# An adaptive-norm block on one core: block transposition over two banks, normalisation on VectorE alone, modulation on VectorE and ScalarE, and another order of the work

## Chip, core and metric

The kernel runs on one core of a Trainium2 chip. The metric is the device time of one execution in microseconds (us). Before the change, five runs took 339.01, 339.18, 339.24, 340.96 and 343.09 us; the median is 339.24.

## What is computed

One row of S = 2048 tokens with D = 640 goes through a transformer block whose scales, shifts and gates come from a condition vector c:

```python
mod = (_silu(c) @ w_mod).reshape(c.shape[0], 6, 1, -1)
sa, ca, ga, sb, cb, gb = (mod[:, 0].copy(), mod[:, 1].copy(), mod[:, 2].copy(), mod[:, 3].copy(), mod[:, 4].copy(), mod[:, 5].copy())
h = _layernorm(x, axis=-1) * (1 + ca) + sa
x = x + ga * _A_ref(h, A_wqkv, A_wo)
h = _layernorm(x, axis=-1) * (1 + cb) + sb
x = x + gb * _B_ref(h, B_w_gate, B_w_up, B_w_down)
```

`_A_ref` is causal attention with 32 heads of 20 and a window of 256 keys. `_B_ref` is a gated layer of width 1536: `sigmoid(h @ w_gate) * (h @ w_up) @ w_down`. Inputs and output are bf16.

## The kernel before

The tokens are cut into 8 chunks of 256, each of two blocks of 128. For a chunk a the work is:

- `ln1` loads the two blocks of x (`load_x`), takes mean and variance (`ln_stats`: bn_stats and bn_aggr on VectorE, L741 and L743), the power -1/2 on GpSimd (POOL, L746 and L748), and normalises in place, (x - mean) * r, at L751. For chunks 0 and 1 the normalised blocks are transposed on TensorE and modulated while they leave PSUM (L786, L787). For chunks 2 to 7 they are transposed by a DMA (L757) into hT, and then modulated there, five instructions a chunk, 256 columns each (`modulate`, L765 on ScalarE, L766 on VectorE or POOL). hT has two buffers.
- `qkv` multiplies hT by the weights of Q, K and V, in groups of five matmuls of 320 columns (`pe_chain`, L658). ScalarE or VectorE copies each group out of PSUM (`evac`, L812 and L813). Q and K are transposed, on TensorE in chunks 0 and 1 (tags qtr, then the copies evqt), by DMA after that.
- `attention` goes through the chunk in two halves of the heads. A half has six sets (three in chunk 0). A set is 8 or 16 score matmuls into the one PSUM tile S (L659), one exponential of 128 x 2048 on ScalarE (L924), and masks on POOL (L932, L934). When all sets of a half are there, a burst of 64 matmuls (32 in chunk 0; "PV") multiplies them by V into two neighbouring PSUM banks X (`burst`).
- `norm` divides the half by its sum: X is transposed in blocks of 32 x 32 into T1 (L975, one instruction for each bank), reciprocal (L980), product (L982), and a transposition back, into On (L984). Four DMAs store it and one loads it again as oT.
- `outproj` multiplies oT by wo and adds x (L1038), then a second norm with the same `ln_stats`, a DMA transposition into h2T and `modulate`. `mlp` runs gate and up matmuls of 256 columns, tanh on ScalarE (L1078), the gated product on VectorE (L1080), the down matmuls, and the addition of x (L1099). Then the block is stored.

PSUM holds S (four banks) and four banks M, which all other groups share, X among them. The gates are multiplied into wo (L1123) and wd (L1064) on VectorE. The three parts of w_mod are loaded into the buffers of wd, wu and hh and multiplied by silu(c) (tags modA, modb, modc).

The order is made when the kernel is built. `Prog.op` records each operation with the engines that may do it, a duration for each, what it reads and writes, and a priority; `Prog.schedule` then places them one after another. It takes, for each engine, the operations that could start within a small margin of the earliest (`PE_EPS` for TensorE, 0.04 for the others), picks of them the one with the lowest priority number, and puts it on the engine where it can start first. A priority is the number written at the call plus the entry of its tag in the table `PRI`:

```python
o.prio = prio + PRI.get(tag, 0.0)
```

Each engine then runs its list strictly in that order, with semaphores between engines. Nearly all DMAs are issued from SP's queue, in such an order too; the bulk loads of weights are chained, so that each waits for the third before it. `port=True` marks operations of VectorE that the placing keeps apart from POOL's. `PACE0` and `PACE` give an earliest time to score sets. The constants that the change touches stand at L399 to L461: `TR1` (used in `norm`, L974 and L977), `XHE` (engines for L751) and `MOE` (engines for `modulate`).

Of the kernel before, what the change touches and what calls it, by code (L numbers as in the profile page):

```python
# [80 lines left out]
class Prog:  # L81
# [67 lines left out]
    def schedule(self):  # L149
# [70 lines left out]
        while placed < n:  # L220
            best = None
            for e in ENGS:
# [21 lines left out]
                if not lst:  # L244
                    continue
                eps = PE_EPS if e == "pe" else 0.04
                pick = min((x for x in lst if x[0] <= tmin + eps), key=lambda x: (x[1].prio, x[1].seq))
# [147 lines left out]
def c_pe(n):  # L395
    return max(n, 64) / 2400.0 + 0.0027


PE_EPS = 0.117  # L399
PRI = {  # L400
    "amodu2": 349.1, "amodu3": 69.8, "amodu4": -2, "amodu5": 20.4, "amodu6": 21.9, "amodu7": 33.4, "apow0": -17.1,
    "apow1": -0.2, "apow2": -233.1, "apow3": -9.4, "apow4": -4.7, "apow5": -39.6, "apow6": -201.2, "apow7": 26.9,
    "astats1": 2, "astats2": -137.3, "astats3": 147.7, "astats4": 52, "astats5": 202.7, "astats6": 112.2,
    "astats7": -8.8, "atr3": -6.2, "atr4": -3.2, "atr5": -194.6, "atr6": 10.3, "atr7": -24.5, "axh0": -203,
    "axh2": -66.7, "axh3": 71.6, "axh4": -24.4, "axh5": 33.9, "axh6": -20.5, "axh7": 9.8, "bmodu0": -166.8,
    "bmodu1": 13.9, "bmodu2": 1.5, "bmodu3": 15.4, "bmodu4": -1.8, "bmodu5": 93.1, "bmodu6": 3.4, "bmodu7": -1.2,
    "bpow0": 4.3, "bpow1": 150.8, "bpow2": -11.8, "bpow3": -188.6, "bpow4": -35, "bpow5": 41.6, "bpow6": -22.5,
    "bpow7": -15.1, "bstats0": 20.1, "bstats1": 21.9, "bstats2": 16.8, "bstats3": 14.9, "bstats4": 25.8,
    "bstats5": -84.4, "bstats6": 22.4, "bstats7": -22.6, "btr0": -39.2, "btr1": -39.3, "btr2": -8.5, "btr3": 35,
    "btr5": -82, "btr6": 4.1, "btr7": -2.4, "bxh0": 24.8, "bxh1": -260.1, "bxh2": -55.1, "bxh3": 34, "bxh4": 72.4,  # L410
    "bxh5": 103.8, "bxh6": 81, "bxh7": 17.1, "divide_0": -16.1, "divide_1": 34.3, "divide_2": -154.9,
    "divide_3": 6.6, "divide_4": 14.8, "divide_5": -19.9, "divide_6": -11.9, "divide_7": 6.6, "down0": -15.1,
    "down1": -21.3, "down2": -20, "down4": 0.4, "down5": 1.9, "down7": 60.2, "evqk0": 16.1, "evqk1": 334.5,
    "evqk2": 27.2, "evqk3": 339.9, "evqk4": -0.3, "evqk5": 4.1, "evqk6": -33, "evqk7": -0.3, "evqt0": -11.6,
    "evqt1": -8.4, "evv0": 41.8, "evv1": 235.3, "evv2": 2.5, "evv3": -5.5, "evv4": -16.9, "evv5": -108.2,
    "evv6": -60.1, "evv7": -59.5, "exp0": -116.1, "exp1": -16.2, "exp2": -46.3, "exp3": 5.9, "exp4": -147.4,
    "exp5": -3.4, "exp6": 1.1, "exp7": -126.7, "glu_0": -1.3, "glu_1": 0.5, "glu_2": 26.7, "glu_3": -19.5,
    "glu_4": -37, "glu_5": -3.6, "glu_6": 8.5, "glu_7": 4.2, "hTe0": -31.6, "hTe1": 34.3, "mask0": 136.2,
    "mask2": -61.4, "mask3": 78.7, "mask4": -36.4, "mask5": -30.5, "mask6": 3.2, "mask7": 94.8, "mlpg0": -25,
    "mlpg1": -24.5, "mlpg2": -24, "mlpu0": -25, "mlpu1": -24.5, "mlpu2": -24, "modb": -25.7, "modc": -22.2,  # L420
    "n_ow_0": -20.3, "n_ow_1": -41.5, "n_ow_2": 44.8, "n_ow_3": 103.9, "n_ow_4": -5.8, "n_ow_5": -19.8,
    "n_ow_6": -1.4, "n_ow_7": 33.8, "oT_0": 17.5, "oT_1": 32.5, "oT_2": 12.6, "oT_3": 76.6, "oT_4": -64.2,
    "oT_5": 13.2, "oT_6": 2.6, "oT_7": 49.3, "out": 7.2, "projk0": -33.4, "projk2": 26.4, "projk3": -3.9,
    "projk4": 15.6, "projk5": 1.5, "projk6": 7.4, "projk7": 4, "projq0": -114.6, "projq2": 45.3, "projq3": -8.2,
    "projq4": 6.1, "projq5": -4, "projq6": 8.5, "projq7": -7.9, "projv0": -43.1, "projv1": 8.7, "projv2": 224.6,
    "projv4": -6, "projv5": 2.7, "projv6": 16.2, "projv7": 10.7, "ptr0": -337.9, "ptr1": -256.9, "pv0": -37.3,
    "pv1": -290.4, "pv2": -37.9, "pv3": -37.1, "pv4": -28.1, "pv5": -70.8, "pv6": -10.1, "pv7": -9.1, "qkt2": 7.9,
    "qkt3": 6.7, "qkt4": 64.8, "qkt5": -12.3, "qkt6": -3.6, "qkt7": -4.9, "qtr0": -154.4, "qtr1": -20.9,
    "recip_1": -1.9, "recip_2": 23.6, "recip_3": -2.4, "recip_4": 28.1, "recip_5": -22.7, "recip_6": 2.1,
    "recip_7": -9.2, "res1_0": -0.2, "res1_1": 5, "res1_2": 55.2, "res1_3": 7.6, "res1_4": 13.1, "res1_5": -5.3,  # L430
    "res1_6": -6.4, "res1_7": 11.2, "res2_0": 6.2, "res2_1": -29.9, "res2_2": -5.9, "res2_3": 1.7, "res2_4": -3.1,
    "res2_5": 40.9, "res2_6": -17.8, "res2_7": 2.6, "score0": -287.1, "score1": -347.7, "score2": -20.2,
    "score3": 1.8, "score4": -13.1, "score5": -50.5, "score6": -2.7, "score7": 11.5, "tanh_0": 29, "tanh_1": 20.7,
    "tanh_2": 23.5, "tanh_3": 22.7, "tanh_4": 26.2, "tanh_6": -2.3, "tanh_7": -20.3, "tr1_0": 19.8, "tr1_1": 6.2,
    "tr1_2": -28.1, "tr1_3": 15.6, "tr1_4": 45.4, "tr1_5": -90.8, "tr1_6": -19.7, "tr1_7": 5.2, "tr2_0": 204.6,
    "tr2_1": 224.6, "tr2_2": -128.4, "tr2_3": 42, "tr2_4": 64.5, "tr2_5": 40.4, "tr2_6": 0.1, "tr2_7": 27.5,
    "wd": -19.6, "wds": -7.7, "wg": 2.8, "wm2": -13.2, "wo": -20, "wo0": -2.2, "wo1": -12.2, "wo2": 9.1, "wo4": 10.8,
    "wo5": 28.7, "wo6": 6.6, "wo7": 30, "wos": -29.2, "x10": 529.8, "x11": 584.9, "x12": 476, "x13": 633,
    "x14": 745.4, "x15": 731.1, "x4": 394.6, "x5": 337, "x6": 375.5, "x7": 0.5, "x8": 473.6, "x9": 471.4, "y0": 10.9,
    "y1": 23.7, "y10": 8.6, "y11": 0.3, "y12": 0.2, "y13": 31.2, "y14": 1, "y15": 2.7, "y2": -0.2, "y3": 0.4,  # L440
    "y4": 24.5, "y5": 24.4, "y6": 15.9, "y7": -3, "y8": 23.9, "y9": 2,
}
TR1 = 2
NPH = 2
NPQ = 2
DEEP = 3
MW = 64
PACE0 = -95.83
PACE = 0.103
AFTER = 0  # L450
LEAD = 2
FILL = 1
# [4 lines left out]
QMAX = 4.5  # L457
PAIR = 0
PAIRO = 0
XHE = ('dve', 'pool')  # L460
MOE = ('dve', 'act', 'pool')  # L461


def build(nc, A_x, A_wqkv, A_wo, B_x, B_w_gate, B_w_up, B_w_down, c, w_mod, out, S=2048):
# [268 lines left out]
    def ln_stats(src, dst, prio, ln, a):  # L733
# [3 lines left out]
        def v(lo, w):  # L737
            return st.ap[:, lo:lo + w]
# [11 lines left out]
        for bi in range(n):  # L750
            A(XHE, lambda e, g, bi=bi: e.tensor_scalar(dst[bi].ap[:], src[bi].ap[:], v(24 + 2 * bi, 1), v(30 + bi, 1),  # L751
                                                       op0=ALU.subtract, op1=ALU.mult), {"dve": 0.44, "pool": 0.95}, port=True,
# [7 lines left out]
    def modulate(dst, sc, sh, Rmod, prio, ln, a):  # L760
        for dt in range(NDT):
            def mo(e, g, dt=dt):
# [3 lines left out]
                return e.tensor_scalar(ap, ap, sc[:, dt:dt + 1], sh[:, dt:dt + 1], op0=ALU.mult, op1=ALU.add)  # L766
            A(MOE, mo, {"dve": 0.34, "act": 0.59, "pool": 0.55}, port=True, reads=[dst.r(("t", bi)) for bi in range(2)] + Rmod, writes=[dst.r(dt)],prio=prio, tag=f"{ln}modu{a}")

# [202 lines left out]
    def norm(X, On, a):  # L971
        T1, Tn, Dr = Tile(p_T1, "T1"), Tile(p_Tn, "Tn"), Tile(p_Dr, "Dr")
        blk = lambda t: t.ap[:].rearrange("p (b r) -> p b r", r=32)[:, :, 0:DH]
        for h in range(2) if TR1 == 2 else ():  # L974
            A("dve", lambda e, g, h=h: e.transpose(T1.ap[:, 512 * h:512 * h + 512], X[h].ap), 0.694, reads=[X[h].r()],  # L975
              writes=[T1.r(h)], prio=3.5, tag=f"tr1_{a}")
        if TR1 == 1:  # L977
            A("dve", lambda e, g: e.transpose(T1.ap[:], Mall[:, X[0].slot:X[0].slot + 2, :].rearrange("p a c -> p (a c)")), 1.23,
# [9 lines left out]
    def attention(a):  # L988
# [20 lines left out]
        for q in range(2):  # L1009
            sets = plan(a)  # L1010
            Es = []
            for si, (ps, md, mf) in enumerate(sets):
                Es.append(score_set(a, q, si, ps, md, mf, PACE0 + PACE * nset[0] if a else 0.0))
                nset[0] += 1
# [167 lines left out]
```

The softmax here doesn't subtract the row's maximum and nothing guards it: scores larger than these inputs give would overflow.

## Time and profile before

The profiled execution took 339.54 us. Its span, from the first to the last instruction of the program, is 337.6 us.

| | busy us | share of the span | instructions |
|---|---|---|---|
| TensorE, matmul (PE) | 327.7 | 97% | 4146 |
| TensorE, weight load (PEld) | 233.1 | 69% | 4146 |
| VectorE (DVE) | 222.2 | 66% | 441 |
| ScalarE (ACT) | 230.0 | 68% | 220 |
| GpSimd (POOL) | 184.1 | 55% | 255 |

| group | count | mean ns |
|---|---|---|
| exponential, ACT, L924 | 90 | 1877 |
| normalisation on DVE, L751 | 26 | 633 |
| normalisation on POOL, L751 | 6 | 2525 |
| modulation of hT on DVE, ACT, POOL | 11, 10, 9 | 611, 591, 576 |
| modulation of h2T on DVE, ACT, POOL | 18, 14, 8 | 429, 590, 564 |
| transposition of one bank, DVE, L975 | 32 | 694 |
| transposition back, DVE, L984 | 16 | 1233 |

How to read it: times are in us unless marked ns. A line such as L751 is a line of the kernel; PE, PEld, DVE, ACT and POOL are the engines, SPq is the queue of DMAs. `x2` counts instructions. In a timeline a row has start, duration, engine, line, operation, what it writes and reads, and in brackets how long the engine stood before it and for whom. A group's "idle before" is the time in which its engine stood just ahead of it. Matmuls are pipelined and their ends are modelled, so a TensorE that is marked busy can still be slower than it could be. The granted clock is the share of TensorE's full clock.

### The profile page before, as it was taken

To read this page: it belongs to the slowest core of one execution; us is meant where nothing else is said; L and a number is where in the kernel's file an instruction comes from. 1 tells how busy PE (TensorE), PEld (TensorE's weight loads), DVE (VectorE), ACT (ScalarE), POOL (GpSimd) and SP (SyncE) were. 2 spreads that over 40 slices of the span, in tenths; PEclk is the share of its full clock that TensorE was granted. 3 is DMA by queue.
4 is the path that set the end of the run, shared out by engine and by line. 5 is a ranking of instruction groups with operands and counts; after the bars stand their busy time and mean duration, and the time that the engine had idled before them with its cause. 6 is when DMAs were issued, how large, how long until landed. Compare 5 with 4: busy or idle time off the path is not lost.

```text
span 337.6 us, 10119 instructions
## 1 busy us (share of the span) xinstructions
PE 327.7 (97%) x4146; PEld 233.1 (69%) x4146; DVE 222.2 (66%) x441; ACT 230.0 (68%) x220; POOL 184.1 (55%) x255
## 2 busy tenths in 40 slices
PE   8998979999999999999999999999999999999996
PEld 3665646666776667766677666776677788887885
DVE  4597768889799767366897376844667662733332
ACT  1597769888998498968799779998699532230120
POOL 4138899775869686656686556665576610100000
PEclk9999979999999999999999999999999999999999
DMA  7988999787980287116871426100140231101101
GB/s 263 375 271 286 249 310 166 139 186 96 231 240 10 67 141 123 46 56 132 119 122 41 91 73 136 39 17 21 60 95 25 60 91 48 21 19 41 41 0 39
DMA packets 71686, 38.72 MB, mean 115 GB/s; under 512 B 46682, under 2 KB 68442, under 8 KB 71642
## 3 DMA queue, kind: packets, MB, share of 16 engines
q1 hardware_dynamic: 71344, 37.76, 46.6%
q8 instruction: 32, 0.52, 0.7%
q10 hardware_dynamic: 298, 0.33, 0.3%
q14 instruction: 12, 0.10, 0.1%
HBM read 21.96 MB, written 5.24 MB: 81 GB/s over the span
## 4 chain that ended last, share of the span: by engine, by line
PE 78%; POOL 9%; DMA 7%; DVE 3%; issue 2%; ACT 1%; ACTq 0%; SPq 0%; POOLq 0%
PE M L658 65%; PE S L659 7%; PE M L659 6%; POOL x L751 3%; DMA x<-in_A_x_dram 3%; POOL E L934 3%; POOL E L932 2%; DMA wo<-in_A_wo_dram 2%; DMA hT<-x 1%; DMA hh<-in_w_mod_dram 1%; ACT E L924 1%; DVE st L741 1%; POOL st L748 1%; DVE x L751 1%; DVE x L1099 0%
## 5 line engine op out<-in xcount | busy, mean ns | idle before, releaser
L924 ACT ACTIVATE E<-S 128x2048 bf16<-128x2048 f32 x90 | 168.9, 1877 | 32.3 <-PE S L659 29.0
L932 POOL TENSOR_SCALAR_AFFINE_SELECT E<-E 128x512 bf16<-128x512 bf16 (+2 forms) x90 | 76.1, 846 | 71.8 <-ACT E L924 68.0
L934 POOL TENSOR_SCALAR_AFFINE_SELECT E<-E 128x512 bf16<-128x512 bf16 (+1 forms) x84 | 69.4, 826 | 0.0
L658 PE MATMUL M<-h2T,wg 128*128 128x256 bf16 x480 | 63.6, 273 | 0.1
L658 PE MATMUL M<-h2T,wu 128*128 128x256 bf16 x480 | 63.2, 273 | 0.0
L1080 DVE SCALAR_TENSOR_TENSOR hh<-sig,M 128x512 bf16<-128x512 f32 x48 | 32.5, 680 | 46.0 <-PE M L658 30.8
L1078 ACT ACTIVATE sig<-M 128x512 f32<-128x512 f32 x48 | 28.5, 594 | 43.9 <-PE M L658 43.9
L658 PE MATMUL M<-wd,hh 128*128 128x320 bf16 (+2 forms) x396 | 55.6, 295 | 0.0
L658 PEld LDWEIGHTS M<-h2T,wg 128*128 128x128 bf16 x480 | 45.0, 98 | 9.6 <-issue 3.0
L658 PEld LDWEIGHTS M<-h2T,wu 128*128 128x128 bf16 x480 | 45.9, 98 | 7.4 <-issue 1.7
L658 PEld LDWEIGHTS M<-wd,hh 128*128 128x128 bf16 x396 | 37.0, 98 | 15.4 <-issue 1.7
L659 PE MATMUL S<-QT,KT 20*128 20x256 bf16 (+1 forms) x960 | 36.1, 246 | 1.8 <-DVE KT L813 1.8
L741 DVE BATCH_NORM_STATS2 st<-x 128x6 f32<-128x320 bf16 x64 | 28.1, 477 | 3.6 <-DMA x<-in_A_x_dram 3.1
L1099 DVE TENSOR_TENSOR x<-M,x 128x320 bf16<-128x320 f32 (+2 forms) x33 | 15.5, 477 | 22.4 <-PE M L658 22.4
L659 PEld LDWEIGHTS S<-QT,KT 20*128 20x128 bf16 x960 | 14.1, 92 | 22.3 <-ACT E L924 16.3
L975 DVE STREAM_TRANSPOSE T<-M 128x512 f32<-128x512 f32 x32 | 21.2, 694 | 12.5 <-PE M L659 12.4
L658 PE MATMUL M<-wk,hT 128*128 128x320 bf16 x160 | 27.1, 309 | 0.0
L658 PE MATMUL M<-wq,hT 128*128 128x320 bf16 x160 | 25.5, 299 | 0.1
L658 PE MATMUL M<-wv,hT 128*128 128x320 bf16 x160 | 25.1, 300 | 0.0
L658 PE MATMUL M<-wo,oT 128*128 128x320 bf16 x160 | 24.7, 300 | 0.0
L659 PE MATMUL M<-E,V 128*32 128x256 bf16 (+1 forms) x960 | 22.8, 246 | 1.4 <-POOL E L934 0.7
L659 PEld LDWEIGHTS M<-E,V 128*32 128x32 bf16 x960 | 20.0, 97 | 5.7 <-issue 2.2
(76 smaller groups left out, 323.2 us busy)
## 6 DMA issues: line engine op xcount, KB each, us to landing
x<-in_A_x_dram SPq DMA_DIRECT2D x30, 160.0 KB
doc<-On SPq DMA_DIRECT2D x64, 40.0 KB
out_dram<-x SPq DMA_DIRECT2D x15, 160.0 KB
wg<-in_B_w_gate_dram SPq DMA_DIRECT2D x5, 384.0 KB
wu<-in_B_w_up_dram SPq DMA_DIRECT2D x5, 384.0 KB
wd<-in_B_w_down_dram SPq DMA_DIRECT2D x4, 480.0 KB
wd<-in_w_mod_dram SPq DMA_DIRECT2D x5, 320.0 KB
wu<-in_w_mod_dram SPq DMA_DIRECT2D x5, 320.0 KB
```

The costliest lines, as they stand in the source:

```text
L658: return e.matmul(o, l, r, start=st, stop=sp, skip_group_check=True)
L659: return e.matmul(o, l, r, start=st, stop=sp, tile_position=tp, skip_group_check=True)
L741: A("dve", lambda e, g, bi=bi, j=j: e.bn_stats(v(bi * 12 + j * 6, 6), src[bi].ap[:, j * 320:(j + 1) * 320]), 0.48, reads=[src[bi].r()], wr ...
L748: A("pool", lambda e, g: e.tensor_tensor(v(30, n), v(28, n), mhalf[:, 0:n], op=ALU.pow), 0.71, reads=[st.r("v"), R_mh], writes=[st.r("r")] ...
L751: A(XHE, lambda e, g, bi=bi: e.tensor_scalar(dst[bi].ap[:], src[bi].ap[:], v(24 + 2 * bi, 1), v(30 + bi, 1), op0=ALU.subtract, op1=ALU.mul ...
L924: A("act", lambda e, eng: e.activation(E.ap[:], Sp.ap[:], ACT.Exp, scale=SM_SCALE), 1.876, reads=[Sp.r()], writes=[E.r()], prio=3, tag=f"e ...
L932: return e.affine_select(ap, ap, pattern=[[0, ap.shape[1]], [1, 128]], compare_op=ALU.is_ge, fill=0.0, base=0, channel_multiplier=-1)
L934: return e.affine_select(ap, ap, pattern=[[0, ap.shape[1]], [-1, 128]], compare_op=ALU.is_ge, fill=0.0, base=-1, channel_multiplier=1)
L975: A("dve", lambda e, g, h=h: e.transpose(T1.ap[:, 512 * h:512 * h + 512], X[h].ap), 0.694, reads=[X[h].r()], writes=[T1.r(h)], prio=3.5, t ...
L1078: A("act", lambda e, g, pg=pg, sg=sg: e.activation(sg.ap[:], pg.ap[:], ACT.Tanh, scale=0.5), c_act(512), reads=[pg.r()], writes=[sg.r()], ...
L1080: A("dve", lambda e, g, pu=pu, sg=sg, f0=f0: e.scalar_tensor_tensor(out=hh.ap[:, f0:f0 + 2, :], in0=sg.ap[:].rearrange("p (a b) -> p a b", ...
L1099: A("dve", lambda e, g, ps=ps, bi=bi, c0=c0, n=n: e.tensor_tensor(x1[bi].ap[:, c0:c0 + n], ps.ap[:, 0:n], x1[bi].ap[:, c0:c0 + n], op=ALU. ...
```

## The change

Three options, three constants and the whole table of priorities change. `TR1 = 1` makes `norm` transpose both banks of X in one VectorE instruction of 1024 columns, in place of one of 512 for each bank. `XHE = ("dve",)` lets only VectorE normalise. `MOE = ("dve", "act")` lets only VectorE and ScalarE modulate. All other operations are the same, on the same engines to choose from; every engine's order is remade, since the table is another one.

```diff
-PE_EPS = 0.117
+PE_EPS = 0.116
...
-TR1 = 2
+TR1 = 1
 NPH = 2
 NPQ = 2
 DEEP = 3
 MW = 64
-PACE0 = -95.83
-PACE = 0.103
+PACE0 = -178.4
+PACE = -4.513
...
-XHE = ('dve', 'pool')
-MOE = ('dve', 'act', 'pool')
+XHE = ("dve",)
+MOE = ("dve", "act")
```

The table has some 200 entries. Those that the prediction speaks of, as the sum of the number at the call and the entry (lower goes first):

| operation (tag) | before | after |
|---|---|---|
| copy of transposed Q or K, chunk 1 (evqt1) | 5 - 8.4 = -3.4 | 5, no entry |
| transposition back, chunk 0 (tr2_0) | 4 + 204.6 = 208.6 | 4 + 13 = 17 |
| statistics of the first norm, chunk 4 (astats4) | 14 + 52 = 66 | 14 - 82.2 = -68.2 |
| load of x for block 6 (x6) | 0.55 + 375.5 = 376.1 | 0.55 + 1.9 = 2.5 |
| load of x for block 7 (x7) | 0.55 + 0.5 = 1.05 | 0.55 + 435.6 = 436.2 |
| load of x for block 8 (x8) | 20.4 + 473.6 = 494 | 20.4 + 850.9 = 871.3 |
| load of the second part of w_mod (wm1) | 0.4, no entry | 0.4 + 79.8 = 80.2 |
| gate and shift products (modb, first and second) | 18 - 25.7 = -7.7, 19 - 25.7 = -6.7 | 40.3, 41.3 |
| the same as columns (modc, first and second) | 18 - 22.2 = -4.2, 19 - 22.2 = -3.2 | 42.3, 43.3 |
| projection of Q, chunks 1 and 3 to 6 | 21, 14.8, 30.1, 21, 34.5 | 52.4, 72.3, 164.8, 126.8, 97.2 |
| projection of K, chunks 1 and 3 to 6 | 21, 19.1, 39.6, 26.5, 33.4 | 57, 55.1, 101.8, 15.9, 206.2 |
| gate and up matmuls, chunks 0 to 7 | 15, 16.5, 18, 43 to 47 | the same |

## Prediction

> **What bounds the kernel now.** I read the page first: busy time, then the slices.
>
> ```profile
> span 337.6 us, 10119 instructions
> ...
> PE 327.7 (97%) x4146; PEld 233.1 (69%) x4146; DVE 222.2 (66%) x441; ACT 230.0 (68%) x220; POOL 184.1 (55%) x255
> ...
> PE   8998979999999999999999999999999999999996
> ...
> PEclk9999979999999999999999999999999999999999
> ```
>
> TensorE is busy in 97% of the span, the others idle a third of it or more. But matmuls are pipelined, and a busy mark is not full speed; so I read the windows next (columns: stretch, length, then busy time and count of PE, PEld, DVE, ACT, POOL, then granted clock, DMA share, GB/s) and counted matmuls.
>
> ```profile
> 40.00:50.00 10.00, 8.20 (x77) 4.58 (x74) 6.91 (x13) 7.27 (x9) 8.30 (x14) 0.83 1.12 335
> ...
> 100.00:110.00 10.00, 10.00 (x110) 6.96 (x109) 9.93 (x22) 8.57 (x7) 10.00 (x11) 1.00 0.05 13
> ...
> 130.00:140.00 10.00, 10.00 (x126) 7.76 (x124) 4.99 (x8) 9.89 (x9) 5.95 (x8) 1.00 0.51 94
> ```
>
> ```profile
> 40.00:45.00 5.00, 3.62 (x34) 2.13 (x31) 3.98 (x6) 4.48 (x6) 3.83 (x8) 1.00 1.05 373
> 45.00:50.00 5.00, 4.58 (x43) 2.45 (x43) 2.93 (x8) 2.79 (x3) 4.47 (x7) 0.66 1.19 296
> ```
>
> Full speed comes from the tail, where TensorE does gate and up matmuls alone: in the timeline one group of 10 starts every 1.09 us (318.46, 319.55, 320.64), 0.109 us for 256 columns, 0.426 ns a column. A matmul of 320 columns is then 0.136 us, one of 128 is 0.055. A score set of 8 or 16 matmuls is a 0.33 us piece in the chain, a PV burst 1.43 to 1.50. In 130 to 140 us TensorE does 38 gate and 38 up matmuls (8.28 us) and 48 score matmuls (4.5 sets, 1.5 us): 9.8 of 10. In that steady state there is nothing to gain. In 40 to 50 us it does 35 projection matmuls (4.77), 8 transposing ones (0.44) and 3 score sets (1.0): 6.2 of 10, so 3.8 us are lost, though "busy" says 8.20. The same count for the other start slices gives 8.6, 8.4, 7.7 and 9.2 of 10 for 10 to 20, 20 to 30, 30 to 40 and 50 to 60 us: 1.4, 1.6, 2.3 and 0.8 lost. So 9.9 us can be won back before 60 us, and hardly anything behind it. A loss can be put anywhere. The timeline of the hole:
>
> ```profile
> 34.22 2.43 SPq L536 DMA_DIRECT2D wg<-in_B_w_gate_dram  x2
> ...
> 36.74 1.21 SPq L757 DMA_TRANSPOSE hT<-x  x1
> ...
> 41.62 1.10 POOL L766 TENSOR_SCALAR hT<-hT,mA 128x256 bf16<-128x256 bf16 x2 [1.17 <-issue]
> ...
> 42.76 0.89 DVE L741 BATCH_NORM_STATS2 st<-x 128x6 f32<-128x320 bf16 x2 [1.02 <-DMA x<-in_A_x_dram]
> ...
> 43.56 1.23 DVE L984 STREAM_TRANSPOSE On<-Tn 128x1024 bf16<-128x1024 bf16 x1
> ...
> 44.71 0.65 DVE L813 CAST KT<-M 128x512 bf16<-128x512 f32 x1
> ...
> 45.42 0.40 PE L659 MATMUL S<-QT,KT 20*128 20x128 bf16 x16 [1.80 <-DVE KT L813]
> ...
> 46.44 1.26 PE L658 MATMUL M<-wk,hT 128*128 128x320 bf16 x4
> ...
> 49.20 5.00 POOL L751 TENSOR_SCALAR x<-x,st 128x640 bf16<-128x640 bf16 x2
> ...
> 60.26 1.50 PE L659 MATMUL M<-E,V 128*32 128x256 bf16 x64 [0.75 <-POOL E L934]
> ```
>
> On the way in, chunk 2's two transposing transfers are issued at 32.80 (right behind its normalisation on POOL, 30.18 to 32.77) and at 36.74 (behind two weight loads on SP's queue, 34.22 to 36.65); they land at 41.5, and POOL modulates from 41.62 to 47.48, in turn with masks. In the hole itself VectorE stands in order: it waits 1.02 us for x of chunk 4 (42.76), does a transposition (1.23 us), and only then the copy of K, 44.71, that the next score set waits for (1.80 us). With projections of chunk 2 behind that set in its own order, TensorE stands, and the granted clock falls to 0.66 in 45 to 50 us. Last, two normalisations hold POOL for 5.0 us from 49.20, the masks queue behind them, and the PV burst at 60.26 waits 0.75 us for a mask. The groups (busy time, mean ns, then idle before):
>
> ```profile
> L975 DVE STREAM_TRANSPOSE T<-M 128x512 f32<-128x512 f32 x32 | 21.2, 694 | 12.5 <-PE M L659 12.4
> ...
> L984 DVE STREAM_TRANSPOSE On<-Tn 128x1024 bf16<-128x1024 bf16 x16 | 19.7, 1233 | 0.1
> ...
> L751 DVE TENSOR_SCALAR x<-x,st 128x640 bf16<-128x640 bf16 x26 | 15.5, 633 | 7.0 <-POOL st L748 6.9
> ...
> L751 POOL TENSOR_SCALAR x<-x,st 128x640 bf16<-128x640 bf16 x6 | 15.1, 2525 | 0.2 <-issue 0.2
> ```
>
> **The change, part by part.** *Normalisation off POOL.* Six of 32 leave POOL, at 2525 ns each, for VectorE, at 594 (the median there; 437 to 1215): POOL loses 15.1 us, VectorE gains 6 x 0.594 = 3.6. One lies right ahead of a transfer (30.18), one at 33.88 waits for a free buffer anyway, two stand ahead of masks at 49.20 and 51.70, two at 101.30 and 105.19. Each comes 2.5 - 0.6 = 1.9 us sooner to what waits; at 32.80 that is worth 0 as long as SP's weight loads hold the second transfer to 36.74.
>
> *Modulation off POOL.* 17 instructions (9 of hT, 8 of h2T, 5.1 + 4.5 us) go to VectorE at 430 ns (median of hT there) or ScalarE at 590. Five are those of the hole: beside the waiting VectorE and ScalarE's gaps they need 5 x 0.43 = 2.2 us behind the transfer, where POOL took 5.9, so chunk 2's projections are ready near 43.8.
>
> *The hole.* It is a matter of order on VectorE (x of chunk 4 and a transposition ahead of the copy of K) and on TensorE (a set ahead of ready projections). Both orders are remade: the copy of K (evqt1) goes from -3.4 to 5, the transposition ahead of it from 208 to 17, the statistics of chunk 4 from 66 to -68; x of chunk 4 keeps the lowest claim on SP's queue (494 to 871). So the statistics may again stand there waiting for x, whose transfer took 3.9 us in the chain (41.53 to 45.45); but projections now can fill in. If the hole goes, it gives 1.8 us and most of the clock, (1 - 0.66) x 5 = 1.7. Ends 0 (the new order stands at the same x) and 3.8 (all that the slice loses); I take 2.5, nearer the upper end because a second source of work is ready 2.6 us sooner.
>
> The Trainium skill, TensorE: Matmul & The Clock Gate, Part 1: The HAM clock gate, says an idle window of about 3.4 us halves the clock; by it a hole of 1.8 us alone should cost no clock, and the sum would win at most 1.8 here. The row shows 0.66 over 5 us, so a drop was paid.
>
> *Masks.* With POOL 5 us freer at 49 to 54 the PV burst at 60.26 need not wait: 0.7 (0 to 0.75). At 101 to 108 the same backlog delays statistics, normalisation on VectorE and an addition, and the PV burst at 114.31 waits 0.55: 0.4 (0 to 0.55).
>
> The Trainium skill, GPSIMD Engine Reference, Engine selection, speaks against the change: an elementwise operation of one input is roughly line rate on GpSimd. At the page's 1.2 GHz, 640 elements would be an estimated 0.53 us there, less than the 594 ns of VectorE's row, and the sum would end with no gain from this part, so near 339. The row says 2525 ns, and the row decides.
>
> *What it costs VectorE.* In 100 to 110 us it is busy 9.93 of 10, and two normalisations (1.2 us) join there; TensorE's evictions (residuals, gated products) queue behind them, and matmuls wait once the four banks are full. I take 0.5 (0 to 1.2). Elsewhere VectorE has room (222 of 337.6 us; the 3.6 and at most 17 x 0.43 = 7.3 more are hidden by its idle time; if that cover were gone they would cost up to 10.9, which only windows as full as that one would bring). On ScalarE the 17 would be 10.0 us, each pushing an exponential back by 0.59; that is slack as long as the last exponential's margin holds (below).
>
> *One transposition over two banks.* 16 times, two of 694 ns (a pair takes 1.31 from its first start) become one. No row has 1024 f32 elements from two banks: the nearest, 1024 bf16 elements, has 1.23; the other end is 2 x 0.694 = 1.39. I take 1.23: 0.08 x 16 = 1.3 us less on VectorE, worth 0 on the path (ends -0.08 and +0.08 each, both hidden). But the first bank is now free after 1.23 instead of 0.69. TensorE's wait for these transpositions is 0.6 us in 3 times in 16 bursts, since two other banks hold two groups (over 2 us) in between; I take 3 x 0.1 = 0.3 (0 to 3 x 0.54 = 1.6).
>
> *The order remade.* New numbers in the table break ties among ready operations; the pacing constant bounds no set before or after (negative throughout). No instruction or DMA is added. SP's queue is reordered: x of block 6 moves ahead (376 to 2.5), block 7 back (1.05 to 436); the w_mod part 1 load goes to 80, still ahead of the x loads; weights keep their chain of three in flight. The gate work (modb, modc) goes from about -7 and -3 to 40 and 43, still ahead of chunk 1's projections at 52 to 63; wo is scaled by 35.5 and first used at about 67 us, so 30 us cover it. The Q and K projections of chunks 3 to 6 fall from 15 to 40 to mostly 55 to 206, behind the gated layers at 15 to 47. Value 0; ends -6.1 (the rest of the start's 9.9 - 3.8 healed) and +6 (the slower rival).
>
> Sum, against the profiled execution's own 339.54 (span 337.6 and 1.94 around it; 0.30 above the median of 339.24): 339.54 - 2.5 - 0.7 - 0.4 + 0.5 + 0.3 = 336.74, less the 0.30: **336.4**.
>
> **The rivals.** *The whole start heals:* the new order also fills 20 to 40 us (1.6 + 2.3 lost): 336.4 - 3.9 = 332.5. For it: those losses are short waits on copies and on POOL. Against: DMA is 0.83 to 1.12 busy there, so data are late, not only order.
>
> *Hidden or given back:* TensorE's work is the same and full behind 60 us; the hole stays, or closes and another of its size opens: 339. For it: x of chunk 4 comes late in either order.
>
> *Slower, by a starved score chain:* a set takes 2.4 us (0.33 score, 1.88 exponential, hand-overs), 90 sets are 216 us in series. The last exponential ends at 266.5; chunk 7 then goes through PV, transfers and its second norm to about 299 us, needs 13.1 + 6.5 us for its layer and 2 to the end, so 321 is possible where 337.6 is real: 16.6 us of margin. If projections wait behind the gated layer of a chunk (19.6 us of TensorE) and the chain starves longer than 16.6, each us beyond it is one us of end. At 22.5 it gives +6: 345. For it: the projections' new numbers. Against: 12 sets of a chunk, 29 us, lie between, and while one works, projections run in its gaps.
>
> **How the numbers follow.** Forecast 0.42 (its own range 334 to 338.5), start healed 0.14, given back 0.17, starved 0.27 (342.7 to 350). A measurement of this kernel can tell 1% from no change: 335.8 and 342.6. Of the forecast case 0.17 lies below 335.8: faster 0.14 + 0.17 = 0.31, same 0.25 + 0.17 = 0.42, slower 0.27. The range leaves out the lowest 0.05 and the upper half of the starved case, about 0.13: 331.5 to 346.
>
> **What would show it.** Right: no normalisation or modulation on POOL, its busy time near 184.1 - 15.1 - 9.6 = 159; clock 1.00 in 45 to 50 us; over 7.5 us of matmuls counted in 40 to 50; one 1.23 us transposition a burst. Wrong: a hole of the same size elsewhere before 60 us (given back); 20 us or more without score sets, the last exponential beyond 283, and a tail with gaps between matmuls (starved); VectorE at 10 of 10 beyond 120 us with TensorE waiting on L1080 or L1099 (its cover gone). A drop of the clock in a stage that now is at 1.00 would alone refute the sum.

## The result, and the profile after

The changed kernel took 340.78 us in the median of 44 runs (338.92 to 343.26), the kernel before 339.32 in 79 runs beside them. The ratio is 1.0044, with a 95% interval of 1.0031 to 1.0057: 0.44% slower, 1.5 us. Medians here and below are of all runs; ratios and the figures by granted clock leave out the runs over 1.5% above the fastest of their kernel (four of 99 of the kernel before, all at a mean clock of 0.995 or less). The profiled execution took 341.01 us, its span is 339.3. The lines of its page that answer to those shown of before:

```profile
span 339.3 us, 10076 instructions
...
PE 327.9 (97%) x4146; PEld 232.5 (69%) x4146; DVE 218.2 (64%) x441; ACT 232.8 (69%) x227; POOL 159.4 (47%) x232
...
PE   8898899999999999999999999999999999999996
...
PEclk9999999999999999999999999999999999999999
```

TensorE is as busy as before (327.9 us), and the clock is 9 or more in every slice, where before had a 7. POOL's busy time fell from 184.1 to 159.4 us, as forecast (159). The slice with the hole, and the one before it, in the windows (columns as above):

```profile
35.00:40.00 5.00, 3.49 (x48) 2.15 (x50) 4.27 (x8) 3.20 (x6) 2.23 (x1) 1.00 1.12 229
40.00:45.00 5.00, 4.51 (x85) 2.71 (x76) 4.62 (x8) 4.16 (x7) 0.41 (x1) 1.00 1.10 335
45.00:50.00 5.00, 5.00 (x60) 3.37 (x60) 4.84 (x14) 5.00 (x6) 2.91 (x6) 1.00 0.78 287
```

From 45 to 50 us TensorE is now busy throughout, at a clock of 1.00. Counted in matmuls, each by its columns at full speed, it does 4.42 us of work there, against 2.43 before, and 8.1 in 40 to 50 us, against 5.9. So the picture that the forecast drew is there, and yet the kernel is slower. The groups show the two prices that were estimated (count, busy time, mean ns, idle before):

```profile
L977 DVE STREAM_TRANSPOSE T<-M 128x1024 f32<-128x1024 f32 x16 | 20.0, 1247 | 16.9 <-PE M L658 16.7
...
L750 DVE TENSOR_SCALAR x<-x,st 128x640 bf16<-128x640 bf16 x32 | 18.1, 597 | 4.0 <-POOL st L747 3.9
```

The long transposition takes 1247 ns (forecast 1230), a normalisation 597 (forecast 594). Where, then, do the 1.5 us come from? I counted TensorE's work up to a given time in every trace in the same way, four small matmuls side by side as one. The table gives how far each trace is ahead of the profiled execution of before, in us of work; single entries are good to some 0.3 (a group that falls just across the mark).

| kernel | by 65 us | by 70 us | by 90 us | end | change from 65 us to the end |
|---|---|---|---|---|---|
| changed | +0.8 | +0.8 | -0.6 | -1.6 | -2.4 |
| changed, second execution (a_again) | +1.9 | +1.8 | +0.3 | 0.0 | -1.9 |
| before, second execution (c_base) | -1.5 | -1.5 | -1.4 | -1.5 | 0.0 |

The change wins in the first 65 us and loses more behind them. The first place of the loss is 65 to 90 us. In the windows of that stretch, before and then after:

```profile
65.00:90.00 25.00, 25.00 (x314) 16.73 (x311) 22.29 (x50) 21.98 (x24) 18.35 (x27) 1.00 0.83 167
```

```profile
65.00:90.00 25.00, 23.79 (x289) 15.47 (x287) 23.33 (x55) 23.06 (x27) 15.68 (x22) 1.00 0.92 186
```

TensorE was never idle there; now it stands for 1.2 us, while VectorE is busy 23.3 of 25 us. (ScalarE is as busy, 23.1, but none of the waits below is for it.) What it waits for, in the list of TensorE's waits of the changed kernel in this stretch (us in total, times, longest; the list of before is empty here):

```profile
PE M L657 <- DVE stg L812: 0.7, 2, 0.4
PE M L658 <- POOL E L933: 0.5, 1, 0.5
```

The second execution of the changed kernel (a_again) has the same waits there, their lengths within 0.01 us. One of them on VectorE's timeline (start, length, engine, line):

```profile
69.84 0.89 DVE L740 BATCH_NORM_STATS2 st<-x 128x6 f32<-128x320 bf16 x2
70.64 0.33 DVE L765 TENSOR_SCALAR hT<-hT,mA 128x256 bf16<-128x256 bf16 x1
70.89 0.20 DVE L742 BATCH_NORM_AGGREGATE st<-st 128x2 f32<-128x12 f32 x1
71.01 0.43 DVE L812 CAST stg<-M 128x320 bf16<-128x320 f32 x1
71.37 0.87 DVE L740 BATCH_NORM_STATS2 st<-x 128x6 f32<-128x320 bf16 x2
72.16 0.47 DVE L812 CAST stg<-M 128x320 bf16<-128x320 f32 x1
72.58 0.89 DVE L740 BATCH_NORM_STATS2 st<-x 128x6 f32<-128x320 bf16 x2
...
73.62 0.75 DVE L750 TENSOR_SCALAR x<-x,st 128x640 bf16<-128x640 bf16 x2
```

The casts L812 take finished projections out of PSUM. The first starts at 71.01, when two statistics (69.84), a modulation (70.64; in before POOL has two of this block's five) and an aggregation are done; the next, at 72.16, stands between further statistics, ahead of two normalisations at 73.62. VectorE has no gap in this stretch, and TensorE has waited 0.30 us for the first cast when it goes on at 71.50. This is the new order more than VectorE's extra work: in a_old (below), with that order but the normalisations and modulations of before on POOL again, the same rows stand ahead of the same cast (71.45), and TensorE waits 0.36 us for it and 0.52 for the mask. Further on it waits 0.4 us at 122 us for a modulation on VectorE, and in this execution, not in the second, 0.7 us at 183 us for the DMA that transposes Q. The last exponential starts at 275.40 us and ends at 277.3, before at 266.5: short of the 283 from which the starved chain would have set the end.

### The profile page after: what moved, and what is told of

It is laid out like the page before. It is cut to its first block, busy times and chain, and to the rows that moved or that the text cites. A ratio compares the mean times of both kernels' runs of the same rounds, so it can differ in the third digit from the quotient of the medians.

```text
span 339.3 us, 10076 instructions
## 1 busy us (share of the span) xinstructions
PE 327.9 (97%) x4146; PEld 232.5 (69%) x4146; DVE 218.2 (64%) x441; ACT 232.8 (69%) x227; POOL 159.4 (47%) x232
## 4 chain that ended last, share of the span: by engine, by line
PE 60%; DMA 1%; SPq 0%; issue 0%; DVE 0%
PE M L657 51%; PE S L658 5%; PE M L658 4%; DMA QT<-stg 1%; SPq L535 0%; DVE x L1098 0%; SPq L756 0%
## 5 line engine op out<-in xcount | busy, mean ns | idle before, releaser
L931 POOL TENSOR_SCALAR_AFFINE_SELECT E<-E 128x512 bf16<-128x512 bf16 (+2 forms) x90 | 78.1, 868 | 104.5 <-ACT E L923 104.4
L933 POOL TENSOR_SCALAR_AFFINE_SELECT E<-E 128x512 bf16<-128x512 bf16 (+1 forms) x84 | 67.2, 800 | 0.0
L657 PE MATMUL M<-h2T,wg 128*128 128x256 bf16 x480 | 62.9, 273 | 0.9 <-DVE h2T L765 0.4
L657 PE MATMUL M<-wd,hh 128*128 128x320 bf16 (+2 forms) x396 | 56.3, 295 | 0.0
L977 DVE STREAM_TRANSPOSE T<-M 128x1024 f32<-128x1024 f32 x16 | 20.0, 1247 | 16.9 <-PE M L658 16.7
L657 PE MATMUL M<-wk,hT 128*128 128x320 bf16 x160 | 26.1, 300 | 0.6 <-DVE KT L812 0.5
```

Of the source, the lines that this page charges most:

```text
L657: return e.matmul(o, l, r, start=st, stop=sp, skip_group_check=True)
L931: return e.affine_select(ap, ap, pattern=[[0, ap.shape[1]], [1, 128]], compare_op=ALU.is_ge, fill=0.0, base=0, channel_multiplier=-1)
L933: return e.affine_select(ap, ap, pattern=[[0, ap.shape[1]], [-1, 128]], compare_op=ALU.is_ge, fill=0.0, base=-1, channel_multiplier=1)
```

## The experiments

All experiments keep the list of each engine's order as the planner made it and alter only what the diff says, between planning and writing out:

```diff
     P.schedule()
+    P.alter()
     P.emit()
```

`place(o, e)` puts an operation into the list of engine e at its planned time. "Order of before" and "order of the change" mean these lists. Every ratio is to the kernel before, run on the same chip.

### The control

`alter` does nothing; the lists are those of before.

> The kernel before, every engine's order as it was, written out through the same frozen order as the single-option kernels: a control for them. If the 0.5 to 0.85% that the single options cost is theirs: ratio to before 1.000, between 0.998 and 1.002. If it is owed to the way in which those kernels were made or to the noise of such small differences: 1.004 or more.

Measured: 339.78 us, ratio 1.0015 (0.9988 to 1.0042). That agrees with 1.000, and it says how little one comparison of this kind can tell apart: some 0.3%. Its trace taught more. Windows of this second execution of the same work:

```profile
10.00:15.00 5.00, 3.36 (x24) 2.09 (x20) 1.88 (x5) 1.58 (x3) 0.81 (x2) 0.70 1.10 374
40.00:45.00 5.00, 5.00 (x81) 3.26 (x81) 3.24 (x6) 4.06 (x7) 4.51 (x6) 1.00 1.05 315
45.00:50.00 5.00, 3.85 (x45) 2.38 (x41) 4.74 (x11) 4.26 (x4) 4.25 (x9) 1.00 1.04 377
```

There is no clock drop at 45 to 50 us. TensorE's wait for the copy of K is there again, but it is 1.1 us long instead of 1.8, and the slice has 3.47 us of work, not 2.43. (Three more kernels below have the order of before in this stretch or nearly so: o_mod, o_tr1 and o_late wait 1.7, 0.6 and 0.7 us for that copy, all at a clock of 1.00; o_mod and o_late do 3.36 us, o_tr1 does 4.15.) And the slice of 5 us shows only half of it: over 40 to 50 us, the stretch that the prediction counted, c_base does 7.8 us of work and o_late, whose lists are those of before up to 62 us, 8.0. The changed kernel does 8.1 and, in its second execution, 8.0; only the profiled execution of before has 5.9. By 50 us c_base stands at -0.5 and o_late at +0.9 against that execution, the changed kernel at +0.2 and +1.0. So in these traces the new order has no gain in the hole over other executions of the old one. The drop of c_base is at 10 to 15 us (0.70), behind a stall of 1.64 us at 11.79 us in which TensorE waits for a normalised x; the trace of before has 0.74 us at the same place and no drop. Later c_base and o_late wait 1.5 us for the mask ahead of the PV burst at 60 us (0.75 in the trace of before). By 65 us the control is 1.5 us behind; from there to the end it changes by 0.0. So the first 65 us differ from one execution to the next, and behind them the order repeats itself here. The stall that the prediction rests on is the order's, in a size that varies; the drop behind it belongs to the execution that was profiled.

The granted clock of all runs says the same. A mean of 0.997 or less was seen in 10 of the 95 runs of the kernel before that stand beside the experiments (median 340.74 us, the others 338.77) and in 6 of 44 of the changed kernel (342.00, the others 340.64). A run with a drop is 1.4 to 2.0 us longer. In the traces a drop is a stretch of 3.4 us at a clock of 0.50 (46.44 to 49.86 in before, 12.04 to 15.46 in c_base), which is worth 1.7. These counts do not show that the change made it rarer.

### One way at a time, in the order of before

o_tr1 replaces each pair of transpositions by one, at the place of the second:

```diff
+for o, p in zip(pairs[::2], pairs[1::2]):
+    p.fn = o.both
+    dve.remove(o)
```

> The order of before is kept; only the two transpositions of a half become one over two banks, at the place of the second. Theory order: 0.999 to 1.001, one of about 1.25 us where a pair took 1.31. Theory VectorE (the first bank is held 0.6 us longer): 1.001 to 1.003 with waits of TensorE for the transposition in more than 3 places.

o_mod takes 17 modulations, o_norm six normalisations off POOL, and o_all3 does all three:

```diff
+for o in [x for x in self.order["pool"] if x.tag[1:5] == "modu"]:
+    self.place(o, max(("dve", "act"), key=lambda e: self.gap(o, e)))
+for o in [x for x in self.order["pool"] if x.tag[1:3] == "xh"]:
+    self.place(o, "dve")
```

> The order of before is kept; only the 17 modulations on POOL go to VectorE or ScalarE, whichever has the larger gap in the plan. Theory order: 0.995 to 1.000, the five of chunk 2 end before 44.5 us instead of 47.5. Theory VectorE: 1.000 to 1.002.

> The order of the kernel before is kept on every engine; only its six normalisations on POOL go to VectorE, each to the place that its planned start has in VectorE's order. Theory order (the options are worth little and the new order cost the 1.5 us): ratio to before 0.996 to 1.001, since POOL is freer at 49 to 54 and 101 to 108 us and the PV bursts at 60 and 114 us wait less. Theory VectorE (a normalisation beside a mask of POOL lasts up to 2.1 us, and evictions stand behind it): 1.002 to 1.005, and a new wait of TensorE for VectorE at 30 to 37 or 101 to 108 us.

> All three options in the order of before. Theory order: 0.993 to 0.999, so faster than the changed kernel by 2 to 4 us, and the new order alone costs that much. Theory VectorE: 1.003 to 1.006, the same as the changed kernel, and the order is worth nothing.

The profiled execution of o_norm took 823 us and tells nothing; o_norm2 is the same kernel in further runs:

> The order of before, six normalisations from POOL to VectorE, once more for its trace. Theory C: level with before within 0.5 us from 105 us to the end, since the last of the six is planned at 99 us; between 65 and 105 us it loses 0.3 to 0.8 us, as the kernel with the options only behind 62 us did at 85 to 100 us; ratio 1.000 to 1.006, by the start. Rival (a normalisation on VectorE costs behind 105 us too, by what it shifts): 1 us or more lost there.

| kernel | median us | ratio, 95% interval | ahead by 65 us | from 65 us to the end |
|---|---|---|---|---|
| o_tr1 | 340.88 | 1.0059 (1.0036 to 1.0082) | +1.3 | -1.8 |
| o_mod | 341.50 | 1.0052 (1.0017 to 1.0087) | +0.6 | -1.3 |
| o_norm | 341.82 | 1.0062 (1.0027 to 1.0097) | no trace | no trace |
| o_norm2 | 341.56 | 1.0075 (1.0036 to 1.0113) | +1.0 | -1.7, all of it by 70 us |
| o_all3 | 341.52 | 1.0085 (1.0058 to 1.0111) | +1.7 | -2.9 |

The theory that the three ways are worth nothing and only the new order costs falls: in the old order each alone is slower by 0.5 to 0.75%, all three by 0.85%. (Against the control's 0.15% the 0.52% of o_mod alone would be within the noise; its trace shows where it loses.) For the long transposition the place is plain. VectorE's and TensorE's timelines of o_tr1:

```profile
161.30 0.49 DVE L1095 TENSOR_TENSOR x<-M,x 128x320 bf16<-128x320 f32 x1 [0.42 <-PE M L714]
161.71 1.24 DVE L1032 STREAM_TRANSPOSE T<-M 128x1024 f32<-128x1024 f32 x1
...
163.01 0.85 PE L714 MATMUL M<-wo,oT 128*128 128x320 bf16 x5 [1.06 <-DVE T L1032]
```

The transposition stands behind an addition, ends at 162.95, and only then are both banks free; TensorE has stood 1.06 us. Before, the first bank came free after 0.69 us of transposing. At 97.4 us it costs 0.41, at 273.8 us 0.20. For the modulations it is the PV burst at 114.28 us, which waits 1.50 us for an addition (0.55 before): the normalisation ahead of that addition starts at 111.92, after 4.17 us in which VectorE waits for its power -1/2 from POOL. For the normalisations the trace shows no loss from 70 us on; the 1.7 us up to there are one stall of 1.78 us at 68.68, ahead of the first matmul on an oT whose load was issued only at 65.95. What they cost lies in the start: 10 of the 17 runs of the two kernels show a mean clock of 0.997 or less, against 10 of 95 before. The five others of o_norm have a median of 339.25 us, near the 338.55 of the 21 such runs of before on that chip. The trace also has a wait of 1.43 us at 39.49 us for the two copies of the gate, behind a product that takes 2.15 us beside a mask of 2.01; o_early (1.45) and o_all3 (1.04) have it too, and the traces in which these early normalisations are on POOL (before, a_pool, a_old) do not. Whether this wait brings on the drop, a trace with a full clock cannot say; it stays open.

### Early or late

The same three ways, but only where the operation is planned before 62 us, or only behind:

```diff
-for o in [x for x in self.order["pool"] if x.tag[1:3] == "xh"]:
+for o in [x for x in self.order["pool"] if x.tag[1:3] == "xh" and x.start < 62]:
```

> The order of before with all three options, but only where their operations are planned before 62 us: four normalisations, the modulations of the second and third block and the first transpositions go to the new way, the rest stays. Theory C: level with before from 65 us to the end within 0.5 us; ratio 0.998 to 1.003, and no gain of 2.5 us by the hole at 45 us, since most executions of before have no clock drop to win back. Rival (the tight VectorE of the start is what costs): ratio 1.005 or more. Second rival (the forecast's: the start heals): 0.993 to 0.996.

> The order of before with all three options, but only where their operations are planned behind 62 us: two normalisations, the later modulations and transpositions go to the new way. Theory C: from 65 us to the end it loses 1.5 to 2.3 us to before (all options in that order lost 2.2), with the wait of TensorE for the long transposition near 163 us; ratio 1.0045 to 1.008. Rival (the start is what costs): ratio 0.998 to 1.002.

o_early: 339.92 us, ratio 1.0041 (1.0011 to 1.0071); from 70 us to the end the count moves by 0.1 at most, and 3 of its 12 runs have a mean clock of 0.997 or less. o_late: 340.59 us, ratio 1.0047 (1.0023 to 1.0071); it is +0.4 at 65 us, -2.1 at the end, with the wait of 1.06 us for the transposition at 164 us again. The late part is as expected, its loss of 2.5 us just above the range. The early part is level in its one trace, and its ratio misses its range: in the median it costs 1.0 us (338.94 before), which must lie ahead of 70 us. So the forecast's reading of the start (0.993 to 0.996) is refuted in the old order, and Theory C's level start as well.

### Undoing one way at a time, in the order of the change

a_again changes nothing, a_tr2 splits the transposition again (last two lines of the diff), a_pool puts six normalisations back on POOL (first two), a_mod seventeen modulations (`xs` are those of one block), a_old does all of it.

```diff
+for o in [x for x in self.ops if x.tag in ("axh3", "axh4", "axh5")]:
+    self.place(o, "pool")
+for o in xs[:n]:
+    self.place(o, "pool")
+h.fn, o.fn = o.half
+dve.insert(dve.index(o), h)
```

> The changed kernel once more, every engine's order as it was: a second execution to look into. Theory C (what TensorE has done by 60 us differs by a microsecond or two from one execution to the next, of either kernel, by when the first loads land; behind 60 us the order repeats, and there the changed kernel always loses): wherever the counted work stands against the trace of before at 65 us, it loses 2.0 to 2.6 us from there to the end (first trace: 2.5); ratio to before 1.002 to 1.007. Rival (the loss is chance too): the loss behind 65 us is under 1 us in this execution.

> The changed kernel with its order, only the transposition split again into two of one bank, back to back at the same place (two of 0.69 for one of 1.25, VectorE 2.2 us more in all, first bank free 0.55 us sooner, second 0.14 later). Theory A with the bank as a main cost (as the single option in the order before, plus 0.59%): ratio to before 1.000 to 1.002. Rival (in its own order, made for it, the one transposition costs nothing): 1.004 or a little above it.

> The changed kernel with its order, only six normalisations (blocks 3, 4 and 5 of the first input, needed 9 us or more after they are made) go back to POOL, at the same place in its queue; VectorE has 3 to 5 us less to do in 33 to 82 us, POOL 15 us more. Theory A with VectorE as the cause between 35 and 90 us: the wait of 1.21 us at 38.3 goes, ratio to before 1.000 to 1.002. Rival (masks on POOL then come late, 2.5 us each time, and the bursts that need them wait): 1.006 or more.

> The changed kernel with its order, only seventeen modulations go back from VectorE and ScalarE to POOL, of the same blocks as in before, the ones that are needed latest. Theory D: loses 1.5 to 2.3 us behind 65 us as the changed kernel, ratio 1.003 to 1.007. Theory E, with the modulations as what costs (the wait of 0.4 us for one on VectorE at 122 us goes): loses 1.0 us or less behind 65 us, ratio under 1.003.

> The changed kernel's order of work with the options of before: two transpositions of one bank, six normalisations and seventeen modulations back on POOL, each at the same place of its queue. What is left of the change is its order. Theory D (in its own order the order is the cost, not the options): from 65 us to the end it loses 1.5 to 2.3 us against the trace of before, as the changed kernel does (1.8 and 2.5), ratio 1.003 to 1.008. Theory E (the options cost in this order too): it loses under 1 us there, ratio under 1.003.

| kernel | median us | ratio, 95% interval | ahead by 65 us | from 65 us to the end |
|---|---|---|---|---|
| a_again | 340.57 | 1.0044 (1.0019 to 1.0068) | +1.9 | -1.9 |
| a_tr2 | 341.57 | 1.0066 (1.0038 to 1.0093) | +1.5 | -1.8 |
| a_pool | 342.11 | 1.0080 (1.0047 to 1.0113) | +0.4 | -1.9 |
| a_mod | 340.22 | 1.0006 (0.9976 to 1.0035) | +2.0 | -3.2 |
| a_old | 342.48 | 1.0098 (1.0062 to 1.0134) | +0.4 | -3.7 |

a_again repeats the ratio to the digit, and the loss behind 65 us. In this order the long transposition costs nothing behind 65 us (a_tr2 loses 1.8 where the change loses 1.9), and the normalisations neither; that the medians of a_tr2 and a_pool lie above a_again's would then come from the first 65 us, which one trace each does not show. a_old keeps nothing of the change but its order and still loses. Of its 3.7 us, 1.2 to 1.6 are my own doing: at 86.73 us TensorE starts, 1.58 us late, on a block whose modulation on POOL, behind a normalisation and two masks, has ended at 86.63; the change waits 0.39 us there. The other 2.1 to 2.5 agree with the loss of the change. a_mod is the one whose ratio and trace disagree: by its ratio it is 0.38 points better than the change and level with before, in its trace it loses more, 2.9 us of it by 90 us. That trace need not stand for its runs: the spans of its twelve runs lie at 336.0 to 336.4 us (four), 337.0 and 337.2, and 338.2 to 338.4 (six), and the trace is one of the longest (338.4); the shortest of before on that chip is 336.1. What the short ones do behind 65 us is not on record. So the traces say that behind 65 us the order of the change costs about 2 us by itself and that undoing the transposition or the normalisations in it does not give this back; for the modulations it stays open, since the times of a_mod say that it may.

### Repairs

a_gbc moves the normalisation at 36.26 us of the changed kernel, which delays TensorE at 39.45. The timeline of the changed kernel there:

```profile
35.98 2.23 POOL L931 TENSOR_SCALAR_AFFINE_SELECT E<-E 128x2048 bf16<-128x2048 bf16 x1 [1.26 <-ACT E L923]
36.26 2.12 DVE L750 TENSOR_SCALAR x<-x,st 128x640 bf16<-128x640 bf16 x1
...
38.30 1.00 DVE L705 TENSOR_SCALAR gbc<-M 128x320 bf16<-128x320 f32 x2
...
39.45 0.77 PE L658 MATMUL M<-E,V 128*32 128x256 bf16 x25 [1.21 <-DVE gbc L705]
```

A normalisation, 430 ns on the mean when POOL rests, takes 2.12 us beside a mask of 2.23 us; the two copies of the gate and the PV burst behind them wait, 1.21 us.

```diff
+n = max(i for i, o in enumerate(dve) if o.tag == "axh3")
+dve.insert(n + 2, dve.pop(n))
```

> The changed kernel with one move: on VectorE the second of the two normalisations at 35 to 38 us goes behind the two copies for which TensorE waited 1.21 us at 38.3. Theory A (the loss is a sum of short waits that VectorE causes, each worth what TensorE stood): about 1.2 us less than the changed kernel, 339.6, ratio to before 1.001. Theory B (score products and exponentials run in step, so a wait healed before 60 us is waited again later): ratio as the changed kernel's, 1.004, within 0.1%, and the work counted on TensorE is ahead of the changed kernel's at 40 us and level with it by 100 us.

Measured: 342.37 us, ratio 1.0094 (1.0059 to 1.0129). The wait of 1.21 us is gone, and the next one is longer. The timeline of a_gbc:

```profile
41.09 0.86 DVE L809 TENSOR_SCALAR hT<-hT,mA 128x256 bf16<-128x256 bf16 x3 [1.65 <-DMA hT<-x]
41.86 0.82 DVE L1025 TENSOR_TENSOR Tn<-T,Dr 128x640 bf16<-128x640 f32 x1
...
42.60 0.69 DVE L856 CAST KT<-M 128x512 bf16<-128x512 f32 x1
...
43.34 0.85 PE L701 MATMUL M<-wk,hT 128*128 128x320 bf16 x5 [2.29 <-DVE KT L856]
```

VectorE now comes to the copy of K at 42.60, behind modulations (41.09), for whose transfer it has stood 1.65 us itself, and a product (41.86), and TensorE waits 2.29 us for it. At 40 us this trace is 2.0 us ahead of the changed kernel's, by 45 us nearly level with it, and by 55 us 0.8 behind. 5 of its 6 runs show a clock of 0.997 or less; the sixth took 340.94 us, near the changed kernel's 340.64 at a full clock. Both theories miss the ratio on the slow side, and why the drop is so frequent here stays open. a_pool gets rid of the same wait, and has 1.3 us for the copy of K and 1.1 us for a mask in its place, between 40 and 51 us.

a_ev pulls the evictions of 62 to 92 us ahead of the statistics:

```diff
+key = {o: o.start - (1.5 if o.tag[:3] in ("evq", "evv") and 62 < o.start < 92 else 0.0) for o in dve}
+dve.sort(key=lambda o: key[o])
```

> The changed kernel with one repair: in VectorE's order the evictions of the projections that are planned between 62 and 92 us stand 1.5 us further ahead, before the statistics and normalisations behind which they waited. Theory C with VectorE as the cause of the first part of the late loss: between 65 and 90 us it loses 0.0 to 0.5 us against before instead of 1.5, keeps that to the end, and the ratio is 1.000 to 1.002. Rival (the exponentials set the pace, and what is won on evictions is waited for at the next score set): the loss behind 90 us grows by as much, ratio 1.003 to 1.006.

Measured: 343.56 us, ratio 1.0123 (1.0083 to 1.0162), the slowest of all. Between 65 and 90 us it loses 3.3 us, by the end 4.2. TensorE's waits in that stretch:

```profile
PE M L701 <- POOL E L976: 1.3, 1, 1.3
PE M L700 <- DVE T L1020: 1.2, 1, 1.2
```

The waits for evictions are gone; in their place TensorE waits 1.2 us for the transposition that frees the banks and 1.3 us for a mask. Both theories miss again. VectorE is busy 23.4 of 25 us there, and what goes ahead in its list pushes back another piece that TensorE needs. No kernel of the study was faster than the one before.

## Why the prediction was wrong

The forecast was 336.4 us, and 340.78 came: the sign was wrong. That the time lies in the range of 331.5 to 346 is owed to the width of the range, not to the mechanism. Step by step:

- *The hole, -2.5.* This is the step that failed first. The row was read rightly, and the hole is closed in the trace after. But its size was that of one execution: over 40 to 50 us two other traces of the old order do 7.8 and 8.0 us of work, two of the new 8.1 and 8.0, and the one that was priced 5.9. Over 7.5 us there, the prediction's sign of being right, is met by the old order too. Also, 85 of 95 runs of the kernel before have a mean clock above 0.997, so for most there was no drop to win back. At 35 to 40 us the new order waits 1.2 and 1.1 us for the copies of the gate. What is left of a gain I estimate from the 1.5 us of the result and the 1.9 to 2.4 us lost behind 65 us: 0.4 to 0.9 us by 65 us, with the mask at 60 us in it, where 3.2 were forecast (2.5 and 0.7).
- *Masks, -0.7 and -0.4.* The wait at 60 us is gone (TensorE busy 5.00 of 5 in 60 to 65 us, before 4.74; the wait was 1.5 us in c_base and o_late), as is the one at 114. In their place stand 0.5 for a mask at 76 us and 0.4 for a modulation at 122. The step held where it looked and said nothing of where the waits went. (Without these two terms the sum would be 337.5, not the 339 that the prediction names.)
- *VectorE's extra work, +0.5 (0 to 1.2).* The place was another: neither trace of the changed kernel has TensorE waiting for VectorE at 100 to 110 us. A cost that goes with the normalisations on VectorE is the wait for the copies of the gate at 39 us, 1.0 to 1.45 us in the traces that have the early ones there ahead of these copies. The 1.2 us of waits at 65 to 90 us are not this term: 0.5 of them are for a mask, and a_old, without the extra work, has the first cast's wait and the mask's too.
- *The bank, +0.3 (0 to 1.6).* In the old order the loss is at the upper end (waits of 1.06 at 163 us, 0.41 at 97 and 0.20 at 274, together 1.67; counted 1.8). In the new order the comparison with a_tr2 shows none.
- *The order, 0 (-6.1 to +6).* The second step that failed: about +2 behind 65 us, most of it in 65 to 90 us, by the traces of after, a_again and a_old; how much of it is the modulations' is open, as said of a_mod. The sentence "A loss can be put anywhere" was right; the sum then gave it the value 0. One reading of the table was wrong too: x of block 6 (2.5) goes ahead of the w_mod load (80.2), not behind it; no run tells what that is worth.
- *The rivals.* The chain did not starve (the last exponential ends at 277.3, the margin at 283). The start did not heal by 6.4 us. "Given back" was the nearest, 339. In the second execution of the changed kernel the lead of 1.9 us by 65 us is 0.3 by 90; it is 1.1 by 115 and gone by 145. Later +0.9 (165 to 180 us) and -0.8 (255 to 285 us) nearly cancel: projections and gated layers come earlier, score sets later. What is lost is more than what was won.

The Trainium skill, GPSIMD Engine Reference, Specifications, says that GpSimd's SBUF interfaces are shared with VectorE and that the two contend when VectorE runs in a two-port mode or has two SBUF inputs. No run here shows which mode a normalisation runs in, but the durations agree with contention: of the 32 normalisations of the changed kernel, the 18 beside which POOL does nothing take 430 ns on the mean, the 14 beside a mask 810 on the mean and up to 2125. The prediction's mean of 594 had such cases in it, but not that the long one decides who waits.

## What to carry to other kernels

Before a hole in a profile goes into a sum, see whether it is in a second execution of the same kernel; here a second look would have taken away most of the largest term of the forecast. One trace can also be of an untypical run, as a_mod's may be: see where its span lies among those of the other runs. Where data arrive just in time, compare kernels by the stretch that repeats (here from 65 us on) and by medians of many runs for the rest. Where one engine is busy 9 of 10 and feeds the bound one in several ways, as VectorE here in 65 to 90 us, moving one piece ahead in its list made another late (a_ev, a_gbc).

## What the hardware showed that I had not expected

A stall of TensorE is not followed by a clock drop every time: 1.80 us ending at 45.42 (before), 1.64 us at 11.79 (c_base) and 1.36 us at 39.45 (a_ev) were followed by 0.66, 0.70 and 0.71 over a 5 us slice, 1.62 us at 11.90 and 1.78 us at 68.68 (o_norm2) and 2.29 us at 43.34 (a_gbc) by 1.00. The stalls of c_base and o_norm2 near 12 us are at the same wait. The Trainium skill, TensorE: Matmul & The Clock Gate, Part 1: The HAM clock gate, calls the window that the gate watches free-running, and says that the number of slow matmuls at a kernel's start varies with its phase. That the same stall acts differently by that phase would fit these rows, but no run here shows the phase. The rows do not agree with its rule that an idle window of about 3.4 us comes before the drop, if the one stall is all that counts.

A stall can also carry "issue" as its reason though a producer is plain: in a_old the 1.58 us ahead of 86.73 end 0.10 us after a modulation on POOL, whose block the matmul reads. And behind 70 us the executions of o_early and before, which share their lists there, agree in TensorE's counted work to 0.1 us at every mark, over 265 us.
